# Loads and stores of half the partitions in pairs from one queue, in pieces of two slots, and a new hand-written order

## The chip, the cores and the metric

The kernel runs on one core of a Trainium2 chip. The metric is the device time of one execution in microseconds (us). A core has five engines with instruction streams of their own: TensorE (PE, matrix products; its weight loads are PEld), VectorE (DVE), ScalarE (ACT), GpSimd (POOL) and SyncE (SP), which here does nothing but issue transfers (DMAs). Each engine runs its instructions in the order in which they were issued, and waits on semaphores for the others.

## The reference

Two branches over S = 2048 tokens of D = 640 channels, mixed by a gate per token:

```python
x = A_q
g = _sigmoid((x * gate_w).sum(-1, keepdims=True))
a = _A_ref(x, A_k, A_v, A_shift_k, A_ssm_k, A_ssm_D)   # q * (longconv(kv, ssm_k) + kv*ssm_D)
b = _B_ref(x, B_w1, B_w2, B_w3, B_w4)
return g * a + (1 - g) * b
```

Branch A: `k_shift` is k convolved along the tokens with four taps per channel, `kv = k_shift * v`, then a causal convolution of kv along all 2048 tokens with `ssm_k` (by FFT in the reference), the term with `ssm_D`, and a product with q. Branch B: layer norm, `w1` (640 to 640), gelu, a shift of each quarter of the channels by 1, -1, 2 or -2 tokens, `w2`, a residual; layer norm, `w3` (640 to 1536), gelu, `w4`, a residual.

## The kernel before

**Layout.** Token t = 32 n + 16 g + s (g is 0 or 1, s from 0 to 15) lies on partition 64 g + n in slot s. So x, k, v, q and out are 128 partitions by 16 slots of 640 channels, and a transfer of one g covers half of the partitions: g = 0 the lower 64, g = 1 the upper 64. For one partition consecutive slots are contiguous in DRAM.

**Work.** `build` lists some 790 tasks. Names used below:

- `sin` and what precedes it make the tables of sines (TRIG). `cjb.j`/`cj.j` spread tap j over all partitions by a product with ones (PE, L464) and copy it out. `fill` holds one PSUM bank for products of zeros (L255), which the launcher issues where it expects PE to wait, so that its clock stays up.
- Branch B: `st1.s` (statistics of a slot: three instructions on DVE, or two activations on ACT), `rs1.s` (POOL), `nm1.s` (normalise), `tr1.s` (10 transposes for two slots, L540), `ev1`/`evh` (copies out of PSUM), `w1.G.p` (five products of 512 columns per part p of a group G of four slots, L615 and L619), `g1.G.p` (gelu on ACT), `w2.s` (L641), `x1.s` (residual, DVE L648), `sq.s`, `ve2`, `st2`, `nm2`, `dt2` (the second norm, with a transpose by DMA), `w3.c.f` (48 of them, L724), `g2`, `w4.s` (L738), `t2.s` (residual, DVE L744), `gate`, `gz`, `gg`.
- Branch A: `trh.cb` (32 transposes of the filter, L754; `evt` copies them out). For each group gi of four slots, from 3 down to 0: four tap products `kvgi.m3..m0` and three additions `kvgi.a2..a0` and the product with v, `kvgi.v` (L774, L778, L782; all on DVE, 128 x 2560). The convolution is a transform of two steps with a trip through DRAM between them: `s1h`/`s1x` (first step of filter and of kv, L809 and L822), `e1` copies, `wF` writes, `rF` reads, `s2` (L856), `e2`, `pa`/`pb` (products on DVE, L871), `s3` (back, L884), `e3`, `wG` writes, `rG` reads, `s4` (L934). `s2` of any part needs all of `wF`, so it needs `s1x.0` to `s1x.3`, which need `kv0.v`. Then `yq.s` (DVE L940) multiplies by q and the gate, `ad.s` (DVE L946) adds branch B, and `st` stores.

**Order.** `ORDER` is a list of task numbers written out by hand; a letter behind a number picks the engine (a: ACT, v: DVE, p: POOL). The tasks are issued in that order, so each engine gets its own sequence from it. `Plan.place` walks the list with assumed durations and chooses PSUM banks and other buffers, and how many products of zeros are put ahead of a PE task; it doesn't move a task.

**Transfers.** All go through `dma` on SP, but for the upper halves of x, which ACT issues. Eight completion semaphores are used in turn: the ninth transfer waits until the first of its turn has landed. Loads come in halves: x in six ranges of slots (two or four slots), k in four ranges of four slots, v in four, q and out in eight of two slots:

```python
for (s0, s1) in [(14, 16), (0, 2), (2, 4), (4, 8), (8, 12), (12, 14)]:
    for g in range(2):
        dma(f"ldx{s0}.{g}", ..., (nc.scalar if g else nc.sync).dma_start(...), queue="ACT" if g else "SP", ...)
```

Each half is a task of its own, and `ORDER` may set the two halves of a range far apart.

Of the kernel before, what the change touches and what calls it, by code (L numbers as in the profile page):

```python
# [16 lines left out]
P = 128  # L17
D = 640
# [23 lines left out]
403 455 48 113a 461 404 405 406 407 408 166 145 168 450a 172 462a 402 46 456a 169 173 443 444a 459 170 167 460a
146 401 171 53 174 152 445 147 447 457 175 153 52 409 414 410 148 458a 137 446a 448a 214 150 151 182 176 149 464
413 415 215 177 183 216a 463 179 180 140 157 451 452 185 143 217 465 473 158 220 163 181 186 159 474a 466a 188
471 416 189 412 164 411 469 477 196 50 221 470a 192 224v 225 218v 478v 472a 197 417 418 467 483 485 193 419 468a
190 486a 191 194 160 484a 154 420 481 161 219 476 165 479 475 195 198 222v 421 155 162 264 424 480a 482a 199 223
# [37 lines left out]
class Plan:  # L84
# [62 lines left out]
    def place(self, order):  # L147
        tasks = self.tasks
        n = len(tasks)
        free = {e: 0.0 for e in LAT}  # L150
# [71 lines left out]
def kernel(  # L222
# [16 lines left out]
    nc = tc.nc  # L239
# [8 lines left out]
    with tc.manual_schedule():  # L248
        nc.vector.memset(env.early("FZ", [P, 512], BF16)[:], 0.0)
# [104 lines left out]
def build(env, nc, io):  # L354
# [19 lines left out]
    def dma(name, nbytes, fn, issue=0.58, queue="SP", **kw):  # L374
        return add(name, queue, issue, fn, nbytes=nbytes, **kw)
# [79 lines left out]
    fill = add("fill", "PE", 0.02, lambda t: None, acq=[ONE], mode="f")  # L455
# [18 lines left out]
    for (s0, s1) in [(14, 16), (0, 2), (2, 4), (4, 8), (8, 12), (12, 14)]:  # L474
        for g in range(2):
            dma(f"ldx{s0}.{g}", 64 * (s1 - s0) * D * BF * 1.2, lambda t, s0=s0, s1=s1, g=g: (nc.scalar if g else nc.sync).dma_start(
                out=env["x"][64 * g:64 * g + 64, s0:s1, :], in_=qv[g, :, s0:s1, :]), queue="ACT" if g else "SP",
                w=[("x", s, g) for s in range(s0, s1)])
# [12 lines left out]
    for (i0, i1) in ((15, 19), (11, 15), (7, 11), (3, 7)):  # L491
        for g in range(2):
            dma(f"ldk{i0}.{g}", 64 * (i1 - i0) * D * BF * HALF, lambda t, i0=i0, i1=i1, g=g: nc.sync.dma_start(
                out=env["K"][64 * g:64 * g + 64, i0:i1, :], in_=kv_[g, :, i0 - 3:i1 - 3, :]),
                w=[("K", i, g) for i in range(i0, i1)], roles=("K",))
    dma("ldkh1", 64 * 3 * D * BF * 2, lambda t: nc.sync.dma_start(out=env["K"][64:128, 0:3, :], in_=kv_[0, :, 13:16, :]),
        w=[("K", i, 1) for i in range(3)], roles=("K",))
    dma("ldkh0", 64 * 3 * D * BF * 2, lambda t: nc.sync.dma_start(out=env["K"][1:64, 0:3, :], in_=kv_[1, 0:63, 13:16, :]),
        w=[("K", i, 0) for i in range(3)], roles=("K",))
# [265 lines left out]
    for gi in (3, 2, 1, 0):  # L765
        for g in range(2):
            dma(f"ldv{gi}.{g}", 64 * 4 * D * BF * HALF, lambda t, gi=gi, g=g: nc.sync.dma_start(
                out=env["VC"][64 * g:64 * g + 64, 0, :, :], in_=vv[g, :, 4 * gi:4 * gi + 4, :]), w=[("V", g)], roles=("VC",))
# [144 lines left out]
    for s0 in range(0, 16, 2):  # L913
# [4 lines left out]
        qown = None  # L918
        for g in range(2):
            def ldq(t, s0=s0, g=g, o=qown):  # L920
                b = (o or t).buf["Q"][0]
                nc.sync.dma_start(out=env["QO"][64 * g:64 * g + 64, 2 * b:2 * b + 2, :], in_=qv[g, :, s0:s0 + 2, :])
            kw = dict(acq=("Q",), after=("W12",)) if qown is None else {}
            t = dma(f"ldq.{s0}.{g}", 64 * 2 * D * BF * HALF, ldq, use=[qown] if qown else [], w=[("q", s0, g)], **kw)
            qown = qown or t
        oown = None
        for i in range(2):
# [14 lines left out]
            y = add(f"yq.{s}", "DVE", 0.88, yq, use=[t], rel=[(t, "U"), (qown, "Q")], r=["GG", ("q", s0, 0), ("q", s0, 1)], acq=("V",),  # L942
# [6 lines left out]
            o = add(f"ad.{s}", "DVE", 0.75, ad, use=[y] + ([oown] if oown else []), rel=[(y, "V")], r=["GG", ("x", s, 0), ("x", s, 1)],  # L949
                    w=[("o", s)], after=("W12",), **kw)  # L950
            oown = oown or o
        for g in range(2):
            def st(t, s0=s0, g=g, o=oown):
                b = 4 + 2 * o.buf["O"][0]
                nc.sync.dma_start(out=ov[g, :, s0:s0 + 2, :], in_=env["QO"][64 * g:64 * g + 64, b:b + 2, :])
            dma(f"st.{s0}.{g}", 64 * 2 * D * BF * HALF, st, r=[("o", s0), ("o", s0 + 1)], rel=[(oown, "O")])
# [32 lines left out]
```

## Time and profile before

| | us |
|---|---|
| median of 3 runs | 238.26 (238.21 to 238.35) |
| the profiled execution | 238.23 |
| its span, first to last instruction | 236.5 |
| outside the span | 1.73 |
| PE busy | 220.1 (93%) |
| DVE busy | 185.9 (79%) |
| ACT busy | 158.2 (67%) |
| POOL busy | 36.8 (16%) |

Transfers move 56.23 MB at a mean of 238 GB/s. The products of zeros count as busy time of PE: 27 of them, 9.7 us, all in the first 24 us. A busy share is an average over stages; which engine bounds a stage is read from the waits in it. PE's mean granted clock is 0.971.

### The profile page before, as it was taken

To read this page: it belongs to the slowest core of one execution; us is meant where nothing else is said; L and a number is where in the kernel's file an instruction comes from. 1 tells how busy PE (TensorE), PEld (TensorE's weight loads), DVE (VectorE), ACT (ScalarE), POOL (GpSimd) and SP (SyncE) were. 2 spreads that over 40 slices of the span, in tenths; PEclk is the share of its full clock that TensorE was granted. 3 is DMA by queue.
4 is the path that set the end of the run, shared out by engine and by line. 5 is a ranking of instruction groups with operands and counts; after the bars stand their busy time and mean duration, and the time that the engine had idled before them with its cause. 6 is when DMAs were issued, how large, how long until landed. Compare 5 with 4: busy or idle time off the path is not lost.

```text
span 236.5 us, 5276 instructions
## 1 busy us (share of the span) xinstructions
PE 220.1 (93%) x2135; PEld 109.7 (46%) x2154; DVE 185.9 (79%) x263; ACT 158.2 (67%) x221; POOL 36.8 (16%) x91
## 2 busy tenths in 40 slices
PE   8489799999999999999999999999879999999990
PEld 2147576634544564444554343334345654454550
DVE  6926696899999989996754888897999327787892
ACT  0995989998699797887963868897976702522000
POOL 8553364000530330000240000000000000000000
PEclk9679999999999989999999999999999999999997
DMA  6999999998998956985999699987851876877942
GB/s 169 206 224 286 288 214 194 229 335 309 358 243 197 257 199 160 271 236 149 320 259 387 205 237 276 259 283 269 262 192 36 316 258 238 294 218 244 266 112 55
DMA packets 37429, 56.23 MB, mean 238 GB/s; under 512 B 13467, under 2 KB 28572, under 8 KB 37404
## 3 DMA queue, kind: packets, MB, share of 16 engines
q1 hardware_dynamic: 36924, 54.57, 80.2%
q10 hardware_dynamic: 480, 1.31, 2.4%
q8 instruction: 17, 0.28, 0.5%
q14 instruction: 8, 0.07, 0.1%
HBM read 34.90 MB, written 18.35 MB: 225 GB/s over the span
## 4 chain that ended last, share of the span: by engine, by line
PE 76%; DMA 13%; DVE 3%; issue 2%; ACT 2%; SPq 1%; ACTq 0%; DVEq 0%
PE PS L724 23%; PE PS L738 16%; PE PS L641 9%; PE PS L615 8%; DMA x<-in_A_q_dram 6%; DMA W<-in_B_w_dram 5%; PE PS L884 4%; PE PS L856 4%; PE PS L809 4%; DMA QO<-in_A_q_dram 2%; PE PS L619 2%; PE PS L754 2%; PE PS L934 2%; DVE W L940 1%; PE PS L540 1%
## 5 line engine op out<-in xcount | busy, mean ns | idle before, releaser
L738 PE MATMUL PS<-W,h2T 128*128 128x128 bf16 (+1 forms) x372 | 53.6, 297 | 0.6
L731 ACT ACTIVATE h2T<-PS 128x512 bf16<-128x512 f32 x48 | 27.8, 605 | 29.6 <-PE PS L724 29.0
L738 PEld LDWEIGHTS <-h2T 128*128 128x128 bf16 x384 | 29.9, 98 | 25.9 <-issue 2.3
L379 ACT CAST FS<-PS 128x1024 bf16<-128x1024 f32 x36 | 35.1, 1017 | 3.6 <-PE PS L809 2.4
L724 PEld LDWEIGHTS <-W 128*128 128x128 bf16 x240 | 21.9, 99 | 30.2 <-issue 8.7
L379 ACT CAST XH<-PS 128x1024 bf16<-128x1024 f32 x26 | 25.6, 1018 | 5.9 <-PE PS L856 4.2
L724 PE MATMUL PS<-x1nT,W 128*128 128x512 bf16 x120 | 29.5, 392 | 0.0
L724 PE MATMUL PS<-XB,W 128*128 128x512 bf16 x120 | 28.3, 380 | 0.0
L774 DVE TENSOR_TENSOR VC<-K,VC 128x2560 bf16<-128x2560 bf16 x16 | 23.7, 1489 | 0.3
L871 DVE TENSOR_TENSOR PP<-XH 128x2048 bf16<-128x2048 bf16 x20 | 23.6, 1220 | 0.5 <-ACT XH L379 0.2
L744 DVE TENSOR_TENSOR x<-PS,x 128x640 bf16<-128x640 f32 x16 | 13.1, 822 | 13.4 <-PE PS L738 13.2
L641 PE MATMUL PS<-W,hsT 128*128 128x128 bf16 (+1 forms) x155 | 23.2, 302 | 0.3
L615 PE MATMUL PS<-xnT,W 128*128 128x512 bf16 x80 | 19.0, 380 | 0.4 <-DMA W<-in_B_w_dram 0.4
L698 POOL TENSOR_TENSOR r<-v,MH 128x2 f32<-128x2 f32 x8 | 8.9, 1107 | 64.7 <-DVE v L693 62.9
L381 DVE CAST XH<-PS 128x1024 bf16<-128x1024 f32 x14 | 16.8, 1221 | 2.7 <-PE PS L856 2.7
L778 DVE TENSOR_TENSOR VC<-VC 128x2560 bf16<-128x2560 bf16 x12 | 17.9, 1490 | 0.3
L940 DVE SCALAR_TENSOR_TENSOR W<-PS,GG,QO 128x640 bf16<-128x640 f32 x16 | 13.4, 880 | 6.0 <-PE PS L934 3.6
L641 PEld LDWEIGHTS <-hsT 128*128 128x128 bf16 x160 | 12.8, 100 | 11.5 <-issue 1.5
L379 ACT CAST GS<-PS 128x1024 bf16<-128x1024 f32 x14 | 13.9, 1016 | 3.2 <-PE PS L884 3.1
L856 PE MATMUL PS<-FX,TRIG 64*32 64x512 bf16 x320 | 12.9, 382 | 1.6 <-DVE GS L381 0.8
L648 DVE SCALAR_TENSOR_TENSOR x<-PS,x 128x640 bf16<-128x640 f32 x16 | 12.8, 819 | 1.0 <-PE PS L641 1.0
L946 DVE SCALAR_TENSOR_TENSOR QO<-x,OG,W 128x640 bf16<-128x640 bf16 x16 | 13.3, 879 | 0.1
(105 smaller groups left out, 266.8 us busy)
## 6 DMA issues: line engine op xcount, KB each, us to landing
FH<-FS SPq DMA_DIRECT2D x8, 640.0 KB, 5.6
FXD<-FS SPq DMA_DIRECT2D x8, 640.0 KB, 4.6
FX<-FH SPq DMA_DIRECT2D x10, 512.0 KB, 4.0
FX<-FXD SPq DMA_DIRECT2D x10, 512.0 KB, 6.0
GX<-GD SPq DMA_DIRECT2D x8, 640.0 KB, 5.2
W<-in_B_w_dram SPq DMA_DIRECT2D x2, 1920.0 KB, 17.4
GD<-GS SPq DMA_DIRECT2D x8, 480.0 KB, 3.7
SK<-in_A_ssm_k_dram SPq DMA_DIRECT2D x5, 512.0 KB, 7.6
```

The lines of the kernel that those rows point to most:

```text
L379: nc.scalar.copy(out=out, in_=in_)
L381: (nc.vector if t.on == "DVE" else nc.gpsimd).tensor_copy(out=out, in_=in_)
L615: nc.tensor.matmul(m[:, b, :], lhsT=W[:, 0, kb, 160 * fb:160 * fb + 128], rhs=rhs(kb, shifts[fb]), start=(kb == 0), stop=(kb == 4))
L641: nc.tensor.matmul(m[:, c0:c1], lhsT=env["hsT"][:, o.buf["hs"][0], fb, 128 * (s % 4):128 * (s % 4) + 128], rhs=env["W12"][:, 1, fb, c0:c1] ...
L724: nc.tensor.matmul(env.PS[:, t.buf["U"][0], :], lhsT=env["W3"][:, kb, 128 * fb:128 * fb + 128], rhs=env.nT(int(nP[-1]))[:, :, kb, :], star ...
L731: nc.scalar.activation(out=env["h2T"][:, o.buf["h2"][0], fb, :], in_=env.PS[:, t.buf["U"][0], :], func=ACT.Gelu_apprx_tanh)
L738: nc.tensor.matmul(m[:, c0:c1], lhsT=env["h2T"][:, o.buf["h2"][0], fb, 128 * (s % 4):128 * (s % 4) + 128], rhs=env["W4"][:, fb, c0:c1], st ...
L774: nc.vector.tensor_tensor(out=VC[:, o], in0=env["K"][:, a + 3 - j:a + 7 - j, :], in1=w, op=ALU.mult)
L778: nc.vector.tensor_tensor(out=VC[:, 1], in0=VC[:, 1], in1=VC[:, 2], op=ALU.add)
L856: nc.tensor.matmul(env.U(t.buf["U"][0])[32 * j:32 * j + 32, gp, :], lhsT=CRI()[64 * gp:64 * gp + 64, 32 * pc:32 * pc + 32], rhs=X[64 * gp: ...
L871: nc.vector.tensor_tensor(out=env["PP"][:, o.buf["PP"][0], a, :].rearrange("p (b c) -> p b c", b=2), in0=X.unsqueeze(1).broadcast_to([P, 2 ...
L940: nc.vector.scalar_tensor_tensor(out=u, in0=env.Uf(t.buf["U"][0])[:, 0:D], scalar=SS("GG")[:, s:s + 1], in1=env["QO"][:, 2 * q.buf["Q"][0] ...
```

## The change

**Halves.** A new helper issues both halves of a range back to back from SP, the upper half first, as one task:

```diff
-HALF = 1.45
+HALF = 1.1
+    def halves(name, nbytes, out, in_, **kw):
+        def fn(t):
+            for g in (1, 0):
+                nc.sync.dma_start(out=out(t, g), in_=in_(t, g))
+        return add(name, "SP", 1.08, fn, nbytes=nbytes, **kw)
-    for (s0, s1) in [(14, 16), (0, 2), (2, 4), (4, 8), (8, 12), (12, 14)]:
...
+    for s0 in (14, 0, 2, 4, 6, 8, 10, 12):
+        halves(f"ldx{s0}", P * 2 * D * BF * HALF, lambda t, g, s0=s0: env["x"][64 * g:64 * g + 64, s0:s0 + 2, :],
...
-    for (i0, i1) in ((15, 19), (11, 15), (7, 11), (3, 7)):
...
+    for i0 in (15, 17, 11, 13, 7, 9, 3, 5):
+        halves(f"ldk{i0}", P * 2 * D * BF * HALF, lambda t, g, i0=i0: env["K"][64 * g:64 * g + 64, i0:i0 + 2, :],
...
+    def kh0(t):
+        nc.sync.dma_start(out=env["K"][1:49, 0:3, :], in_=kv_[1, 0:48, 13:16, :])
+        nc.sync.dma_start(out=env["K"][49:64, 0:3, :], in_=kv_[1, 48:63, 13:16, :])
...
+        for h in range(2):
+            halves(f"ldv{gi}.{h}", P * 2 * D * BF * HALF, lambda t, g, h=h: env["VC"][64 * g:64 * g + 64, 0, 2 * h:2 * h + 2, :],
...
+        qown = halves(f"ldq.{s0}", ..., acq=("Q",), w=[("q", s0)], after=("W12",))
+        halves(f"st.{s0}", ..., r=[("o", s0), ("o", s0 + 1)], rel=[(oown, "O")])
```

x goes from 12 transfers (6 on SP, 6 on ACT) to 16 on SP, k from 8 to 16 plus one for the split of `ldkh0`, v from 8 to 16; q and out stay at 16 each, now two by two. ACT issues none.

**Zeros.** The memset of the zeros becomes a task (`zeros`, on DVE, behind one small memset), and at least one product of zeros is put ahead of each `cjb`:

```diff
+                    if self.kept is not None and t.name[:3] == "cjb":
+                        t.fill = max(t.fill, 1)
-        nc.vector.memset(env.early("FZ", [P, 512], BF16)[:], 0.0)
+    zeros = add("zeros", "DVE", 0.3, lambda t: nc.vector.memset(env.early("FZ", [P, 512], BF16)[:], 0.0), roles=("C0",))
```

The assumed durations of `ad` (0.75 to 0.88) and of the first free moment of SP (0 to 0.58) change too; they act on `place` alone.

**Order.** `ORDER` is new as a whole, and the numbers stand for other tasks, since there are 769 instead of 788. Read back into names, the sequences begin like this (a name of a half pair stands for two transfers after the change):

```
SP before  ldD ldx14.1 ldx14.0 ldCJ ldx0.1 ldx2.0 ldx2.1 ldx12.1 ldx8.1 ldx4.1 ldx0.0 ldgw ldsk0 ldw2b0 ldw2b3 ldw2b2
 (and ACT) ldsk3 ldx4.0 ldw2b1 ldsk4 ldx12.0 ldsk2 ldw1 ldx8.0 ldsk1 ldw2a ldk15.0 ldk7.1 ldk11.1 ldk3.1 ldk15.1
           ldkh0 ldk11.0 ldk3.0 ldv3.1 ldk7.0 ldv3.0 ldw4 ldw3 wFh.4.1 ...
SP after   ldx0 ldsk2 ldCJ ldx14 ldx4 ldsk4 ldx2 ldD ldsk3 ldw2b3 ldsk1 ldsk0 ldx6 ldw1 ldgw ldk17 ldw2b0 ldx8 ldw2b2
           ldx10 ldx12 ldkh1 ldk15 ldv3.0 ldk13 ldk7 ldk5 ldw2a ldkh0 ldv3.1 ldw2b1 ldk11 ldk3 ldw3 wFh.4.0 wFh.4.1 ...
PE before  fill cjb x4 trh.0 trh.3 tr1.2 tr1.14 tr1.0 trh.2 w1.0.0 tr1.4 w1.0.2 trh.4 trh.1 w1.0.4 w1.0.1 w1.0.3 tr1.6
           tr1.12 w2.0 w2.2 w2.1 tr1.8 ...
PE after   fill cjb x4 trh.4 trh.2 trh.3 tr1.0 tr1.14 trh.0 trh.1 tr1.2 tr1.4 w1.0.0 w1.0.2 s1h.4 s1h.6 w1.0.4 w1.0.3
           s1h.0 s1h.1 tr1.6 w1.0.1 s1hr.0 s1h.3 w1.1.0 tr1.8 w1.1.2 s1h.7 s1hr.4 w1.1.4 w1.1.1 w1.1.3 s1h.2 s1h.5
           w2.2 w2.0 w2.5 w2.4 w2.3 ...
DVE before ... evt.4 evh.0 nm1.7 nm1.13 st1.10 ev1.6 st1.11 dfold x1.0 x1.2 x1.1 nm1.10 nm1.11 ev1.8 x1.3
           kv3.m3 kv3.m2 kv3.a2 ...
DVE after  ... evt.1 st1.8 nm1.7 dfold st1.9 nm1.8 nm1.6 kv3.m2 ev1.6 nm1.9 st1.12 st1.11 ev1.8
           kv3.m3 kv3.a2 kv3.m1 kv3.a1 kv3.m0 x1.2 x1.0 x1.5 ...
ACT before st1.15 st1.3 cj.3 cj.2 cj.0 cj.1 sin evt.0 st1.5 ev1.14 evt.3 evt.2 st1.6 g1.0.0 ...
ACT after  st1.0 st1.1 cj.2 cj.0 cj.3 sin evt.4 evt.2 st1.4 nm1.3 ev1.14 evt.0 st1.6 ev1.4 g1.0.0 ...
```

Around the first of the last four slots of kv, `s1x.0`, PE's order changes too. Ahead of it stood, before, w3.0.8, w3.1.0, w3.1.5, w3.1.10 and w4.1; they now stand behind it, and no task goes the other way. On DVE 58 tasks stood from kv3.m3 to kv0.v (32 of kv, 12 x1, 6 nm2, 5 ve2, e1h, gz, gg); now 53 (31 of kv, 15 x1, 2 nm1, 2 ve2, ev1, gz, nm2). In the section from the first s2 to the last s3 PE has 16 w3 and 4 w4 besides before, and 23 w3 and 4 w4 after. PE's sequence changes the shape of its products 101 times before and 118 times after, 62 and 72 of them behind `s1x.0`.

More of the change, by code (lines that the diff above doesn't have):

```diff
@@ L42 @@
[L42 to L46, printed above, removed]
@@ new lines @@
+73v 396a 52 37 393 392a 71v 33 66v 35 34 55v 81v 74 65v 24 79a 56v 67 394v 28 57 68v 69v 19 72 76a 40 75v 58a
+59v 387 389 388a 82 84v 30 89v 87a 25 80 32 90 83v 88 77 85 86a 26 27 78v 119 120 390v 123 47 124 39 450 454
+451a 455a 398 127 95v 96 92v 125 397 438 97v 42 99v 91v 440 126 43 441a 46 128 439a 93 29 121 122 446 447a 98
+401 94v 444 100v 141 142 111v 101 145 456 105v 48 445a 102v 146 457a 458 149 150 459a 399 31 41 400 106 143 147
+148 112 442 144 402 403 404 405 452 453a 113a 45 114 135 136 129 154 151 103a 115a 49 130 155 108v 138 443a 104
@@ new lines @@
+286 552a 287 545 582 556 310 554a 281 558 288 308 583 557v 559a 585 560 561 271 304 282 311 325 571 586a 584v
+572 272 326 562 312 210 277 566 573v 567 587 343 564a 569 315 278 563v 568a 588 316 574 575a 603 619 630 570v
+589a 590 614 323 329 324 576 591v 707 577 330 546 350 331 547v 620 592 548a 332 615 617 333 635 317 618a 616v
+593 621a 334 318 578 579a 313 580v 598 314 622 604 606 549 605a 319 623a 327 624 599 320 344 345v 646 651 607v
+328 594 695 351v 600a 581 625 631 595v 696v 596a 633 321 632v 601 565 634a 602a 636 283 637v 626 322 597 638 284
@@ L66 @@
+639a 608 609 628a 335 353v 627a 662 663 664a 640 336 610 612a 641 611a 678 289 667 652 654 347v 275 655a 613
+653v 647 649 650a 341 629 648v 668 290 656 665 269 276 657 666a 342 679 681 279 683 680a 270 280 669v 346 658
+348 660a 682v 672 670 293 671a 684 659a 673 685a 642 643a 294 644v 674 354 686 676a 661 687a 688 689 675a 337
+338 690 691v 339 645 295 692a 677 693 352 340 291 296 355 697 702 292 699 363 703 700 706 708 733 701 715 711
[4 rows of a table added]
 """
@@ L149, in place @@
         n = len(tasks)
-        free = {e: 0.0 for e in LAT}
+        free = {e: 0.0 if e != "SP" else 0.58 for e in LAT}
         bufs = {p: [0.0] * k for p, k in self.pools.items()}
@@ L372, in build, with dma @@
         qv, kv_, vv, ov = tok(q2), tok(k2), tok(v2), tok(o2)
-    def dma(name, nbytes, fn, issue=0.58, queue="SP", **kw):
-        return add(name, queue, issue, fn, nbytes=nbytes, **kw)
+    def dma(name, nbytes, fn, issue=0.58, **kw):
+        return add(name, "SP", issue, fn, nbytes=nbytes, **kw)
+    def halves(name, nbytes, out, in_, **kw):
[3 more added lines that the diff above has]
+        return add(name, "SP", 1.08, fn, nbytes=nbytes, **kw)
     def copy(t, out, in_):
@@ L453, in build @@
     add("sin", "ACT", 3.5, c_sin, r=["pha", "c0"], w=["TRIG"], roles=("PRE", "C0"))
-    fill = add("fill", "PE", 0.02, lambda t: None, acq=[ONE], mode="f")
+    zeros = add("zeros", "DVE", 0.3, lambda t: nc.vector.memset(env.early("FZ", [P, 512], BF16)[:], 0.0), roles=("C0",))
+    fill = add("fill", "PE", 0.02, lambda t: None, use=[zeros], acq=[ONE], mode="f", roles=("C0",))
     dma("ldCJ", 5120, lambda t: nc.sync.dma_start(out=env.early("CJR", [1, 4 * D], BF16), in_=io["sk"].rearrange("d j -> (d j)").unsqueeze(0)),
@@ L471, in build @@
                                                   in_=io["gw"].rearrange("(t p) -> p t", p=P)), w=["GW"])
-    for (s0, s1) in [(14, 16), (0, 2), (2, 4), (4, 8), (8, 12), (12, 14)]:
[L475 to L478, printed above, removed]
+    for s0 in (14, 0, 2, 4, 6, 8, 10, 12):
+        halves(f"ldx{s0}", P * 2 * D * BF * HALF, lambda t, g, s0=s0: env["x"][64 * g:64 * g + 64, s0:s0 + 2, :],
+               lambda t, g, s0=s0: qv[g, :, s0:s0 + 2, :], w=[("x", s, g) for s in (s0, s0 + 1) for g in range(2)])
     dma("ldw1", 819200, lambda t: nc.sync.dma_start(out=env["W12"][:, 0], in_=io["w1"].rearrange("(t p) n -> p t n", p=P)),
@@ L490, in build @@
             w=[("SK", cb)], roles=("SK",))
-    for (i0, i1) in ((15, 19), (11, 15), (7, 11), (3, 7)):
[L492 to L496, printed above, removed]
+    for i0 in (15, 17, 11, 13, 7, 9, 3, 5):
+        halves(f"ldk{i0}", P * 2 * D * BF * HALF, lambda t, g, i0=i0: env["K"][64 * g:64 * g + 64, i0:i0 + 2, :],
+               lambda t, g, i0=i0: kv_[g, :, i0 - 3:i0 - 1, :], w=[("K", i, g) for i in (i0, i0 + 1) for g in range(2)], roles=("K",))
+    dma("ldkh1", 64 * 3 * D * BF * HALF, lambda t: nc.sync.dma_start(out=env["K"][64:128, 0:3, :], in_=kv_[0, :, 13:16, :]),
         w=[("K", i, 1) for i in range(3)], roles=("K",))
-    dma("ldkh0", 64 * 3 * D * BF * 2, lambda t: nc.sync.dma_start(out=env["K"][1:64, 0:3, :], in_=kv_[1, 0:63, 13:16, :]),
-        w=[("K", i, 0) for i in range(3)], roles=("K",))
+    def kh0(t):
+        nc.sync.dma_start(out=env["K"][1:49, 0:3, :], in_=kv_[1, 0:48, 13:16, :])
+        nc.sync.dma_start(out=env["K"][49:64, 0:3, :], in_=kv_[1, 48:63, 13:16, :])
+    dma("ldkh0", 64 * 3 * D * BF * HALF, kh0, issue=1.08, w=[("K", i, 0) for i in range(3)], roles=("K",))
     dma("ldw3", 1966080, lambda t: nc.sync.dma_start(out=env["W3"][:], in_=io["w3"].rearrange("(t p) n -> p t n", p=P)), w=["W3"])
@@ L765, in build @@
     for gi in (3, 2, 1, 0):
-        for g in range(2):
-            dma(f"ldv{gi}.{g}", 64 * 4 * D * BF * HALF, lambda t, gi=gi, g=g: nc.sync.dma_start(
-                out=env["VC"][64 * g:64 * g + 64, 0, :, :], in_=vv[g, :, 4 * gi:4 * gi + 4, :]), w=[("V", g)], roles=("VC",))
+        for h in range(2):
+            halves(f"ldv{gi}.{h}", P * 2 * D * BF * HALF, lambda t, g, h=h: env["VC"][64 * g:64 * g + 64, 0, 2 * h:2 * h + 2, :],
+                   lambda t, g, gi=gi, h=h: vv[g, :, 4 * gi + 2 * h:4 * gi + 2 * h + 2, :], w=[("V", h)], roles=("VC",))
         a = 4 * gi
@@ L917, in build @@
         ld = dma(f"rG.{s0}", P * 5120, rg, issue=0.5, r=[("G", m) for m in range(10)], acq=("GX",), after=("FX",))
[L918 to L925, printed above, removed]
+        qown = halves(f"ldq.{s0}", P * 2 * D * BF * 1.3, lambda t, g: env["QO"][64 * g:64 * g + 64, 2 * t.buf["Q"][0]:2 * t.buf["Q"][0] + 2, :],
+                      lambda t, g, s0=s0: qv[g, :, s0:s0 + 2, :], acq=("Q",), w=[("q", s0)], after=("W12",))
         oown = None
@@ L941, in yq @@
                                                in1=env["QO"][:, 2 * q.buf["Q"][0] + i, :], op0=ALU.mult, op1=ALU.mult)
-            y = add(f"yq.{s}", "DVE", 0.88, yq, use=[t], rel=[(t, "U"), (qown, "Q")], r=["GG", ("q", s0, 0), ("q", s0, 1)], acq=("V",),
+            y = add(f"yq.{s}", "DVE", 0.88, yq, use=[t], rel=[(t, "U"), (qown, "Q")], r=["GG", ("q", s0)], acq=("V",),
                     after=("C0",))
@@ L948, in build @@
             kw = dict(acq=("O",)) if oown is None else {}
-            o = add(f"ad.{s}", "DVE", 0.75, ad, use=[y] + ([oown] if oown else []), rel=[(y, "V")], r=["GG", ("x", s, 0), ("x", s, 1)],
+            o = add(f"ad.{s}", "DVE", 0.88, ad, use=[y] + ([oown] if oown else []), rel=[(y, "V")], r=["GG", ("x", s, 0), ("x", s, 1)],
                     w=[("o", s)], after=("W12",), **kw)
             oown = oown or o
[L952 to L956, printed above, removed]
+        halves(f"st.{s0}", P * 2 * D * BF * 1.3, lambda t, g, s0=s0: ov[g, :, s0:s0 + 2, :],
+               lambda t, g, o=oown: env["QO"][64 * g:64 * g + 64, 4 + 2 * o.buf["O"][0]:6 + 2 * o.buf["O"][0], :],
+               r=[("o", s0), ("o", s0 + 1)], rel=[(oown, "O")])
     pl.close()
```

31 lines of the change are left out of this document (11 added, 20 removed), and 8 rows, old and new, of the table ORDER.

## The prediction

> **What bounds the kernel now.** I read the busy times by stage first.
>
> ```profile
> core 0: us, PE busy (x) PEld busy (x) DVE busy (x) ACT busy (x) POOL busy (x), PEclk, DMA share, GB/s
> 0.00:27.00 27.00, 19.66 (x161) 11.34 (x163) 18.04 (x49) 17.68 (x23) 14.94 (x46) 0.87 0.95 225
> 27.00:160.00 133.00, 132.52 (x1245) 63.86 (x1254) 112.48 (x154) 111.03 (x164) 21.85 (x46) 0.99 0.91 255
> 160.00:180.00 20.00, 17.74 (x324) 8.60 (x327) 17.54 (x17) 16.08 (x19) 0.00 (x0) 1.00 0.63 212
> 180.00:216.00 36.00, 35.84 (x303) 18.07 (x304) 23.05 (x27) 13.42 (x18) 0.00 (x0) 1.00 0.75 253
> 216.00:230.50 14.50, 14.37 (x110) 7.84 (x110) 12.98 (x17) 0.00 (x0) 0.00 (x0) 1.00 0.64 179
> 230.50:236.50 6.00, 0.00 (x0) 0.00 (x0) 1.77 (x3) 0.00 (x0) 0.00 (x0) 0.72 0.23 55
> ```
>
> From 27 us on PE idles 3.0 us in all (0.48 + 2.26 + 0.16 + 0.13), so PE bounds the kernel from there to its last product at 230.5. In the first 27 us it is busy for 19.66, of which 9.7 are zeros: some 17 us without useful work. The last 6.0 us are the last residual, sum and stores. The chain of waits says what that start waits for:
>
> ```profile
> 5.06 9.59 DMA x<-in_A_q_dram
> ...
> 16.20 10.76 DMA W<-in_B_w_dram
> 26.96 0.05 issue
> 27.01 1.25 PE PS L615 x5
> ```
>
> w1's first products wait for W1, which lands at 26.96, late in a transfer queue with a DMA share near 1. Next, the timelines of DVE and of PE around branch A:
>
> ```profile
> 45.60 2.89 DVE L774 TENSOR_TENSOR VC<-K,VC 128x2560 bf16<-128x2560 bf16 x2
> ...
> 107.87 1.49 DVE L782 TENSOR_TENSOR K<-VC 128x2560 bf16<-128x2560 bf16 x1 [0.88 <-DMA VC<-in_A_v_dram]
> ```
> ```profile
> 111.31 0.82 PE L809 MATMUL PS<-K,TRIG 64*128 64x512 bf16 x6
> ```
>
> DVE works from kv3.m3 at 45.60 to the end of kv0.v at 109.36, 63.8 us with 0.88 of waiting. PE reaches s1x.0, which needs kv0.v, at 111.31. So DVE is second in line by only 1.95 us: a PE that runs ahead gains that much, and no more unless DVE's chain ends earlier. Last, what halves move at, from the stages table of other stretches:
>
> ```profile
> 2.50:6.00 3.50, 3.50 (x12) 1.21 (x11) 2.87 (x11) 0.43 (x1) 3.34 (x10) 1.00 1.00 271
> 30.00:36.00 6.00, 6.00 (x90) 4.51 (x91) 5.80 (x15) 5.36 (x11) 4.34 (x12) 1.00 1.04 213
> 36.00:42.00 6.00, 5.95 (x53) 3.73 (x53) 3.85 (x9) 5.64 (x7) 2.33 (x6) 1.00 1.03 198
> 50.00:56.00 6.00, 6.00 (x61) 2.27 (x61) 5.86 (x5) 5.18 (x9) 0.00 (x0) 1.00 1.06 386
> ```
>
> The last column is GB/s, the one before the DMA share; all four are saturated. From 30 to 42 us halves of k come in runs of one half: about 205. From 2.5 to 6 upper and lower halves of x come mixed, from two queues: 271. From 50 to 56 whole weights: 386.
>
> **The change part by part.**
>
> *The start of PE.* Up to and with W1, 5.38 MB stood in the queue; now 5.12 MB. ACT issued x until 5.53 and ran its first activation at 6.86, behind a table load of 1.28; x's first pair lands at about 4.6 (as in before: 4.40 for its first pair), and the table load needs no data, so ACT starts up to 2.3 us earlier. Both let w1.0.0 start at 24 to 26 instead of 27.01, I take 25, and by then two more trh (3.7 us, from L754's 3.77 for two) and tr1.4 (0.6) are done. PE's work from w1.0.0 to s1x.0 was 84.3 us (27.01 to 111.31). It loses these 4.3 and the five tasks that go behind s1x.0: four w3 (1.10 each, 5.50 for 25 products in the chain) and a w4 (3.3), 7.7. Left are 72.3: with no wait PE would be at s1x.0 at 97.3.
>
> *k and DVE.* DVE's kv3.m3 now needs slots 11 to 14, so pair ldk11, behind 10.00 MB in the queue (before, 10.08 MB had landed at 47.99 by the trace's landings). From 47.9 I subtract: k and v up to there, 2.62 MB, at 271 instead of 205 (12.8 to 9.7): 3.1. Half of x, 1.3 MB, came in runs of upper halves: 1.5. Three filter loads now stand in a row, 1.57 MB: at 386 instead of the 225 of 10 to 20 us they would save 2.9; they still share the ports with x around them, so half, 1.5. Sum 6.1: S, the start of kv3.m3, is 41.8. Bounds: none of it (47.9), and all of it with the other half of x too (38.8). DVE alone would be there at 38.4 (ldk13, behind 7.75 MB, at about 37.0 less 4.5, then 5.9 us: kv3.m2 1.49, ev1 twice 0.82, nm1 0.43, two st1 of 1.17), so it would wait 3.4 us. What queues behind that wait: x1.2, which frees the bank pair that PE's fifth w2 needs. It ends five kv operations later, at 41.8 + 7.5 + 0.8 = 50.1; PE would be there at 25 + 20.4 (ten w1, ten s1h, two tr1, four w2) = 45.4. PE waits 4.7 and comes to s1x.0 at 102.0.
>
> From kv3.m3 to kv0.v DVE had 63.8. One kv operation (1.49), five nm2 (2.2), three ve2 (0.9), e1h (1.22) and gg (0.34) go, three x1 (2.5), two nm1 (0.9) and ev1 (0.82) come: 61.9. x1.12 and x1.13 come so soon that they may wait for PE's w2, 0 to 1.5, I take 0.8. kv0.v ends at 41.8 + 61.9 + 0.8 = 104.5, after PE's 102.0: **s1x.0 now waits for DVE**, and runs at 104.7.
>
> *From s1x.0 to the end.* Before: 230.47 - 111.31 = 119.2. Added: the five tasks, 7.7. Ten more changes of shape in PE's sequence: a stretch of s2 costs 0.34 for 8 products and 0.77 for 24, so 0.125 for the stretch; two changes make one stretch, 0.6 to 1.25, I take 0.9. In the transform section PE idled 2.36 us (55.64 busy of 128 to 186, DVE 49.65); seven w3 more there (7.7) against some 4.8 us more on DVE should remove half of it: -1.2, bounds 0 and -2.4. Sum 119.2 + 7.7 + 0.9 - 1.2 = 126.6.
>
> *Edits at nothing.* SP issues 27 more transfers at about 0.5: 14 us of a queue that waits for some 140 us in its own waits view; 51 must go before ldk11 is complete, 26 us of 41.8. Without that cover each would cost its 0.5. Eight in flight at 164 KB are 1.3 MB, 4.8 us at 271, more than the 3.0 of x's quickest landing. One product of zeros ahead of each tap product is at most 4 x 0.61; PE waited 3.45 for ACT there, and even 2.4 us late would end in PE's wait for x1.2. The memset moves by about 0.3 on a DVE that waits for x soon after. q and out keep their 16 + 16 transfers, and the last stores their two. v in more pieces: 0 to 1 us, DVE waited 0.88 for it once already. ldkh0 is needed only by the last taps.
>
> *Sum.* 41.8 + 61.9 + 0.8 + 0.2 + 126.6 = 231.3 for PE's end; with 6.0 and the 1.73 outside the span 239.0, against 238.23 of the profiled execution (0.03 under the median). The break-even is S at 41.0.
>
> **The rivals.** *Early k (faster).* Pairs run well above 271 (202 to 206 us, q and out, moves 340), all terms count, S is 39.0; DVE hardly waits, and the transform section loses all its idle time: 239.0 - 2.8 - 1.2 = 235.0. For it: PE's 17 useless us at the start, and a timing that only 2.8 us of transfers decide. Against: the row at 2.5 to 6 had two queues, this has one, where a run of one half can still form.
>
> *Halves serialise (slower).* If pairs on one queue still move at 205, only the filter's 1.5 is saved, S is 46.4 and the time 239.0 + 4.6 = 243.6; it decides as soon as pairs stay under about 240 GB/s. The rows of 30 to 42 speak for it, those of 2.5 to 6 against. The Trainium skill, DMA: Bandwidth & Descriptors, Rules for kernel authors, says this of transfers to disjoint partition halves: "Don't bother — they serialize"; by that rule the time is this rival's. The trace agrees for runs of one half and not for mixed ones (271 against 205).
>
> *New stalls in the transform section (slower).* DVE's 54.5 us and the copies on ACT sit in a section of some 64; with two buffers each for the s2 results and products, its waits could double rather than halve: +2.4 + 1.2, 242.6.
>
> **How the numbers follow.** Forecast 0.42, early k 0.33, serialised halves 0.12, transform stalls 0.13. The forecast's own range is S from 40.4 to 43.4: 237.6 to 240.6. Measurement tells 0.2%, 0.48 us, from no change: of the forecast's 0.42, 0.05 are faster, 0.11 the same, 0.26 slower. Faster: 0.05 + 0.33 = 0.38; same 0.11; slower 0.26 + 0.12 + 0.13 = 0.51. The range reaches from the fast rival at 235.0, slightly below for its own unknowns, to the transform rival at 242.6: 234.6 to 242.6, leaving out most of the serialised case.
>
> **What would show it.** In the changed profile: W1 landed before 26 us and w1.0.0 at 24 to 26; DVE's L774 after its first operation waits on K, and five operations in a row start at about 41.8; PE waits at L641 for an x1 near 45 to 50; and at L809, near 102 to 105, for L782. If PE finds kv0.v done at s1x.0, the forecast is wrong, and so it is if the k pairs land at 205 GB/s or over 300, or if PE idles over 2.4 us between s2 and s3.

## The result and the profile after

The changed kernel takes 239.96 us (median of 12 runs), the kernel before 237.73 (12 runs beside them): a ratio of 1.0105, interval 1.0068 to 1.0141, so about 1% slower. The prediction said 239.0 and slower. Against the kernel before, it had forecast 0.8 us more; found are 1.8 for the profiled executions and 2.2 for the medians. The profiled execution took 240.0, with a span of 238.2. Here and below medians are of all executions, while ratios leave out those in a second, slower state of the chip, into which the profiled executions of the first two experiments fell.

The same stages as before (columns as there; the last stretch shown ends with PE's last product, now at 232.4):

```profile
core 0: us, PE busy (x) PEld busy (x) DVE busy (x) ACT busy (x) POOL busy (x), PEclk, DMA share, GB/s
0.00:27.00 27.00, 24.85 (x246) 15.82 (x247) 20.64 (x51) 21.36 (x28) 17.07 (x48) 0.94 0.89 252
27.00:160.00 133.00, 126.34 (x1229) 57.49 (x1228) 112.08 (x152) 108.74 (x163) 24.68 (x43) 0.99 0.86 256
160.00:180.00 20.00, 20.00 (x259) 9.06 (x265) 15.49 (x16) 14.42 (x18) 0.00 (x0) 1.00 0.52 159
180.00:216.00 36.00, 36.00 (x324) 17.47 (x300) 23.20 (x28) 11.95 (x17) 0.00 (x0) 1.00 0.77 255
216.00:232.40 16.40, 15.74 (x122) 8.31 (x120) 13.57 (x18) 0.60 (x1) 0.00 (x0) 1.00 0.53 148
```

The start is better: PE is busy for 24.85 us of the first 27, not 19.66. Of that, 10.6 are products of zeros (34 of them), 9.7 before, so the useful work there rose from some 10 to some 14 us. The transform stage is better too: no idle time from 160 to 180, where there were 2.26 us. But from 27 to 160 PE now idles 6.7 us, where it had idled 0.5. The view of PE's waits names them:

```profile
PE PS L650 <- DVE x L657: 3.6, 1, 3.6
PE PS L818 <- DVE xnT L390: 1.5, 1, 1.5
...
PE PS L865 <- DMA FX<-FH: 1.2, 1, 1.2
...
PE PS L818 <- DVE K L791: 0.3, 1, 0.3
```

The first is `w2.3` waiting for `x1.2`, the second an `s1h` behind `kv3.m2`, the last `s1x.0` for `kv0.v`. The chain of waits shows what stands behind them (start, length, engine and line; SPq is SP issuing a transfer):

```profile
5.42 5.77 DMA SK<-in_A_ssm_k_dram
...
12.99 9.37 DMA GW<-in_gate_w_dram
22.99 0.59 SPq L383
...
31.24 0.60 SPq L383
35.94 6.68 DMA K<-in_A_k_dram
42.64 1.50 DVE VC L783
...
50.16 0.84 DVE x L657 x2
51.03 4.57 PE PS L650 x20
...
103.76 1.50 DVE K L791
105.31 0.61 PE PS L818 x4
```

From 13 to 36 us it runs over SP. W1, which lands at 21.82, holds a semaphore turn, and SP issues nothing from 19.75 until then. Then one issue follows another, until the second half of ldk11 goes out at 35.94 and lands at 42.6. (The chain names the gate weights, issued right behind W1, whose small load lands at 22.36. But SP's timeline has no gap behind 21.84, so their turn cost nothing.) SP's timeline at W1's turn, and DVE's at `kv3.m3`:

```profile
18.20 1.55 SPq L493 DMA_DIRECT2D W<-in_B_w_dram  x1
21.84 2.38 SPq L383 DMA_DIRECT2D x<-in_A_q_dram  x4
```
```profile
42.64 1.49 DVE L783 TENSOR_TENSOR VC<-K,VC 128x2560 bf16<-128x2560 bf16 x1 [4.06 <-DMA K<-in_A_k_dram]
```

DVE's `kv3.m3` starts when k has landed. It had been ready 4.06 us earlier. Everything up to `x1.2` comes behind it, and PE stands. After that stall PE's clock is low for 4 us (PE alone; busy, granted clock, DMA share, GB/s):

```profile
50.00:52.00 2.00, 0.96 (x4) 0.94 1.06 397
52.00:54.00 2.00, 2.00 (x10) 0.50 1.06 361
54.00:56.00 2.00, 2.00 (x20) 0.70 1.08 361
```

That is 1.0 + 0.6 us more. (Before had a dip of the same worth at 86 to 90, 0.58 and 0.57, without such a stall. So from 27 to 160 us the mean clock is 0.99 in both, and that the stall caused this dip is not shown.) The rates of the pairs:

```profile
2.50:6.00 3.50, 3.39 (x12) 1.22 (x11) 3.22 (x14) 1.37 (x2) 3.33 (x8) 1.00 0.96 303
22.00:30.00 8.00, 8.00 (x91) 4.81 (x90) 7.36 (x18) 7.16 (x11) 3.47 (x10) 1.00 0.79 216
28.00:32.00 4.00, 4.00 (x39) 1.23 (x37) 2.50 (x8) 3.99 (x6) 2.42 (x6) 1.00 0.98 253
30.00:36.00 6.00, 4.48 (x39) 1.97 (x36) 3.30 (x6) 6.00 (x8) 1.14 (x3) 1.00 0.96 271
```

From 28 to 32 little but pairs is under way (until 29.3 also ldkh1, 240 KB): 253 GB/s, and 271 and 303 in the rows where other loads lie between them. Runs of one half, in pieces of four slots, had moved at 198 to 213. From 22 to 30 the share is only 0.79: there the transfers wait for SP.

### The profile page after: what moved, and what is told of

It reads as the page before. It is cut to its first block, busy times and chain, and to the rows that moved or that the text cites. A ratio compares the mean times of both kernels' runs of the same rounds, so it can differ in the third digit from the quotient of the medians.

```text
span 238.2 us, 5341 instructions
## 1 busy us (share of the span) xinstructions
PE 222.9 (94%) x2159; PEld 108.1 (45%) x2159; DVE 186.7 (78%) x262; ACT 157.1 (66%) x224; POOL 41.7 (18%) x90
## 4 chain that ended last, share of the span: by engine, by line
PE 60%; DMA 17%; DVE 10%; SPq 8%; issue 2%; ACT 1%; DVEq 0%; ACTq 0%
PE PS L747 21%; PE PS L733 15%; SPq L383 6%; PE PS L650 6%; PE PS L865 5%; DMA GW<-in_gate_w_dram 4%; PE PS L893 4%; PE PS L624 4%; DVE VC L787 4%; DMA GX<-GD 4%; DVE VC L783 3%; DMA K<-in_A_k_dram 3%; DMA FX<-FH 3%; DMA SK<-in_A_ssm_k_dram 2%; PE PS L937 2%
## 5 line engine op out<-in xcount | busy, mean ns | idle before, releaser
L747 PE MATMUL PS<-W,h2T 128*128 128x512 bf16 (+1 forms) x384 | 53.9, 300 | 0.0
L388 ACT CAST FS<-PS 128x1024 bf16<-128x1024 f32 x38 | 37.3, 1023 | 3.4 <-PE PS L818 2.4
L733 PEld LDWEIGHTS <-W 128*128 128x128 bf16 x240 | 21.0, 98 | 30.5 <-issue 9.3
L388 ACT CAST XH<-PS 128x1024 bf16<-128x1024 f32 x25 | 24.9, 1014 | 9.4 <-PE PS L865 8.5
L733 PE MATMUL PS<-XB,W 128*128 128x512 bf16 x120 | 29.0, 381 | 0.0
L650 PE MATMUL PS<-W,hsT 128*128 128x512 bf16 (+1 forms) x160 | 25.1, 313 | 3.6 <-DVE x L657 3.6
L733 PE MATMUL PS<-x1nT,W 128*128 128x512 bf16 x120 | 28.1, 380 | 0.0
L880 DVE TENSOR_TENSOR PP<-XH 128x2048 bf16<-128x2048 bf16 x20 | 24.2, 1221 | 2.8 <-ACT XH L388 1.6
L390 DVE CAST XH<-PS 128x1024 bf16<-128x1024 f32 x15 | 18.2, 1221 | 3.9 <-PE PS L865 2.5
L707 POOL TENSOR_TENSOR r<-v,MH 128x2 f32<-128x2 f32 x8 | 7.8, 978 | 68.2 <-DVE v L702 56.5
```

The costliest lines, as they stand in the source:

```text
L388: nc.scalar.copy(out=out, in_=in_)
L390: (nc.vector if t.on == "DVE" else nc.gpsimd).tensor_copy(out=out, in_=in_)
L650: nc.tensor.matmul(m[:, c0:c1], lhsT=env["hsT"][:, o.buf["hs"][0], fb, 128 * (s % 4):128 * (s % 4) + 128], rhs=env["W12"][:, 1, fb, c0:c1] ...
L733: nc.tensor.matmul(env.PS[:, t.buf["U"][0], :], lhsT=env["W3"][:, kb, 128 * fb:128 * fb + 128], rhs=env.nT(int(nP[-1]))[:, :, kb, :], star ...
L747: nc.tensor.matmul(m[:, c0:c1], lhsT=env["h2T"][:, o.buf["h2"][0], fb, 128 * (s % 4):128 * (s % 4) + 128], rhs=env["W4"][:, fb, c0:c1], st ...
L880: nc.vector.tensor_tensor(out=env["PP"][:, o.buf["PP"][0], a, :].rearrange("p (b c) -> p b c", b=2), in0=X.unsqueeze(1).broadcast_to([P, 2 ...
```

## The experiments

My theory: the arrival of k for `kv3.m3` sets `s1x.0`, through DVE's chain and through `x1.2` and PE; and k comes late for its place in SP's queue, not for its rate. The rivals: PE's stall is a loss by itself; what lies behind `s1x.0` sets the end; the transfers' rate sets k's arrival. A part of the changes below is a new place in `ORDER`, told in the names of tasks.

**k earlier.** Order in SP's queue:

```diff
-ldkh1 ldk15 ldv3.0 ldk13 ldk7 ldk5 ldw2a ldkh0 ldv3.1 ldw2b1 ldk11 ldk3
+ldk15 ldk13 ldk11 ldv3.0 ldkh1 ldk7 ldk5 ldw2a ldkh0 ldv3.1 ldw2b1 ldk3
```

> Only the order in SP's queue differs from the changed kernel: ldk11 is issued right behind ldk13, and ldv3.0, ldkh1, ldk7, ldk5, ldw2a, ldkh0, ldv3.1 and ldw2b1 come after it. Theory (the arrival of k for kv3.m3 holds DVE's chain to s1x.0 and, through x1.2, PE): kv3.m3 starts when DVE is ready, at 37 to 39 instead of 42.64; PE's wait for x1.2 falls from 3.6 us to under 1; s1x.0 starts at 101 to 102.5 instead of 105.3; the time is 2.5 to 4 us under the changed kernel's 239.96, so 236 to 237.5. Rival (what lies behind s1x.0 sets the end): s1x.0 comes earlier, but the us gained there are given back as waits in the transform section, and the time is within 0.7 us of 239.96.

Measured: 237.27 us, ratio to the kernel before 0.9963 (0.9920 to 1.0005). `kv3.m3` starts at 37.51 without a wait. But `s1x.0` comes at 104.26 only, a gain of 1.05 us. PE's waits, and the one on its timeline:

```profile
PE PS L650 <- DMA W<-in_B_w_dram: 3.4, 2, 3.0
```
```profile
46.68 7.76 PE L650 MATMUL PS<-W,hsT 128*128 128x512 bf16 x46 [3.02 <-DMA W<-in_B_w_dram]
```

The old wait is replaced by one for W2, whose last part I had moved behind more loads: it lands at 46.64. The time is as expected, the way to it is not: a second load is as urgent as k.

**x1 earlier on DVE.**

```diff
-kv3.m3 kv3.a2 kv3.m1 kv3.a1 kv3.m0 x1.2 x1.0
+kv3.m3 kv3.a2 x1.2 kv3.m1 kv3.a1 x1.0 kv3.m0
```

> Only DVE's order differs from the changed kernel: x1.2 runs behind kv3.a2 and x1.0 behind kv3.a1, instead of both behind the five kv3 operations. Both kernels give DVE the same work up to kv0.v. Theory (DVE's chain from kv3.m3 to kv0.v sets s1x.0): PE's wait of 3.6 us for x1.2 goes, but comes back at s1x.0 as a wait of 3 to 5.5 us for kv0.v; s1x.0 stays at 105 +- 0.5 and the time within 0.5 us of 239.96. Rival (PE's stall at w2 and the lower clock behind it are the loss themselves): the time falls by 3.6 to 5.3 us, to 234.7 to 236.4.

Measured: 240.66, ratio 1.0080 (1.0033 to 1.0127), against 1.0105 for the changed kernel; `s1x.0` at 105.43. The stall of 3.6 broke up into waits of 1.50, 1.07 and 0.71. The rival's 234.7 to 236.4 did not come, so the stall is not the whole loss by itself: with k late, PE loses the time in one place or another. The wait did not come back at `s1x.0`, as I had expected (0.34 there). In this profile k came later still (`kv3.m3` at 44.84, not 42.64) and `s1x.0` hardly so; whether the new place of x1 wins back a part of the stall, these runs don't tell, since the intervals of the two ratios overlap.

**k first, W2 next.** As the first experiment, and ldw2a and ldw2b1 right behind ldk11:

```diff
-ldk15 ldk13 ldk11 ldv3.0 ldkh1 ldk7 ldk5 ldw2a ldkh0 ldv3.1 ldw2b1 ldk3
+ldk15 ldk13 ldk11 ldw2a ldw2b1 ldv3.0 ldkh1 ldk7 ldk5 ldkh0 ldv3.1 ldk3
```

> As e1_k_early, with ldw2a and ldw2b1 put right behind ldk11 in SP's queue, ahead of ldv3.0, ldkh1, ldk7 and ldk5. In e1_k_early kv3.m3 started at 37.5 as expected, but PE then waited 3.4 us for W2a and W2b1, and s1x.0 came only 1.05 us earlier than in the changed kernel. Theory (the order of the loads in SP's queue is what costs: k, then W2): both waits are gone, PE idles under 1 us between 27 and 60, s1x.0 starts at 99.5 to 101 instead of 105.3, and the time is 234 to 236, faster than before. Rival (PE and DVE wait for each other at x1 and w2 whatever the loads do): DVE's waits for PE's w2 grow to over 3 us again, s1x.0 stays later than 103 and the time is 236.5 or more.

Measured: 234.51 us, ratio 0.9873 (0.9831 to 0.9915): faster than both kernels. PE's largest waits, then `kv3.m3` on DVE and `s1x.0` on PE:

```profile
PE PS L865 <- DMA FX<-FH: 1.5, 1, 1.5
PE PS L256 <- DVE C L464: 1.2, 1, 1.2
PE PS L865 <- DMA FX<-FXD: 0.7, 1, 0.7
```
```profile
37.73 1.48 DVE L783 TENSOR_TENSOR VC<-K,VC 128x2560 bf16<-128x2560 bf16 x1
```
```profile
99.09 0.60 PE L818 MATMUL PS<-K,TRIG 64*128 64x512 bf16 x4 [0.34 <-DVE K L791]
```

PE waits nowhere between 27 and 99 us. `s1x.0` is 6.2 us earlier than in the changed kernel. The same code, the same transfers, the same order on PE and DVE: a few places changed in one queue turn 1% slower into 1.3% faster. The first theory stands, with W2 beside k.

**One transfer for each pair.** For the loads of x, k, v and q:

```diff
-            for g in (1, 0):
-                nc.sync.dma_start(out=out(t, g), in_=in_(t, g))
+            for g in (None,) if name[:2] == "ld" else (1, 0):
+                nc.sync.dma_start(out=out(t, g), in_=in_(t, g))
```

(g = None: all 128 partitions, from a source with the two halves as its outermost dimension.)

> As the changed kernel, but each pair of halves of x, k, v and q is one transfer of 128 partitions instead of two of 64; same bytes, same order, 36 issues fewer on SP, 21 of them ahead of ldk11's last. Theory (SP's issuing, 0.64 us for each half, back to back from 21.8 to 36.5 us, sets when k lands): ldk11 lands at 34 to 38 instead of 42.6, kv3.m3 starts at 36 to 39, and the time falls by 2.5 to 4 us to 236 to 237.5. Rival (the transfers themselves set it, at some 270 GB/s whatever the number of issues): ldk11 lands within 1 us of 42.6 and the time stays within 0.5 us of 239.96. A second rival (a transfer over all partitions of such a source is no faster than one half): rates near 205 GB/s in the same stretches, ldk11 later than 44, slower than 241.

Measured: 379.51 us, ratio 1.597 (1.590 to 1.604). All three expectations missed. A stretch in which nothing but such loads ran, and SP's part of the chain there:

```profile
69.00:75.00 6.00, 0.00 (x0) 0.00 (x0) 0.00 (x0) 0.00 (x0) 0.00 (x0) 0.50 0.13 51
```
```profile
68.97 6.36 SPq L387
75.37 7.02 SPq L387
82.44 6.22 SPq L387
```

51 GB/s at a share of 0.13, which is 2 of 16 DMA engines, and each issue takes 6 to 7 us of SP instead of 0.6. The Trainium skill, DMA: Bandwidth & Descriptors, Why a DMA increments its semaphore by 16 and not by 1, says that the number of engines is the largest up to 16 that divides the slowest dimension on both sides; for a source whose slowest dimension is 2 that gives 2, and the trace agrees. So in this form one transfer can't stand in for a pair, and the run, which was to test SP's pace, says nothing on it.

**W1 from ACT's queue.** One load issued by another engine:

```diff
-    dma("ldw1", 819200, lambda t: nc.sync.dma_start(out=env["W12"][:, 0], ...
+    dma("ldw1", 819200, lambda t: nc.scalar.dma_start(out=env["W12"][:, 0], ..., queue="ACT", ...
```

> As the changed kernel, but W1 is issued from ACT, just ahead of its sine, instead of from SP. Theory (SP is held: its issue behind W1 waits for the semaphore turn that W1 holds until it lands at 21.8, and from there 23 issues of 0.64 us set when k lands): SP is not held at 21.8, the DMA share from 22 to 30 us rises from 0.8 to over 0.9, ldk11 lands 1.5 to 4 us earlier than 42.6, and the time falls by 1 to 3 us to 237 to 239. Rival (eight in flight or the bytes set the pace, whichever engine issues): ldk11 lands within 1 us of 42.6 and the time is within 0.5 us of the changed kernel.

Measured: 242.08, ratio 1.0180 (1.0136 to 1.0224), so neither. The semaphores' turns run over both queues. W1 took a turn at 9.18 and SP met it sooner, with the next half of x. SP's timeline, and the transfers in the gap:

```profile
9.82 2.31 SPq L497 DMA_DIRECT2D SK<-in_A_ssm_k_dram  x2
19.07 1.11 SPq L383 DMA_DIRECT2D x<-in_A_q_dram  x2
```
```profile
18.00:22.00 4.00, 4.00 (x56) 3.22 (x55) 0.90 (x1) 2.23 (x6) 1.77 (x5) 1.00 0.33 87
```

SP stands from 12.1 until W1 lands at 19.06, the transfers run dry (share 0.33), `kv3.m3` comes at 45.07 instead of 42.64 (+2.4), `s1x.0` at 107.70 (+2.4), and the median is 2.1 us longer. This was not the test that I had meant. It shows the hold of SP; what the hold costs it does not show, since with a change as small as the lower half first (below) `kv3.m3` came at 44.95 and the ratio was 1.0160.

**The small edits undone.** Lower half first, no zeros at the taps, ldkh0 as one transfer; then the first two of them alone; then the changed kernel again as their measure:

```diff
-            for g in (1, 0):
+            for g in (0, 1):
-                    if self.kept is not None and t.name[:3] == "cjb":
-                        t.fill = max(t.fill, 1)
-        nc.sync.dma_start(out=env["K"][1:49, 0:3, :], in_=kv_[1, 0:48, 13:16, :])
-        nc.sync.dma_start(out=env["K"][49:64, 0:3, :], in_=kv_[1, 48:63, 13:16, :])
+        nc.sync.dma_start(out=env["K"][1:64, 0:3, :], in_=kv_[1, 0:63, 13:16, :])
```

> The changed kernel with three of its small edits undone at once: the lower half is issued first again, no product of zeros is forced ahead of each tap product, and ldkh0 is one transfer again. The prediction put all of these at nothing: the time stays within 0.5 us of 239.96, kv3.m3 within 0.7 us of 42.6 and w1's first product within 0.4 of 26.1. Rival (the zeros keep PE's clock up, or the order of the halves counts): w1's first product later than 26.5, or a time that differs by over 0.7 us.

> As the changed kernel, with the lower half of each pair issued first, as before. e4_small_undone (three small edits undone at once) was about 0.9% slower than the changed kernel. If the order of the halves is the cause, this one is at 241 to 242.5 with kv3.m3 near 44; if not, it stays within 0.5 us of 239.96.

> As the changed kernel, without the product of zeros forced ahead of each tap product. If the zeros at the taps are the cause of e4_small_undone's 0.9%, this one is at 241 to 242.5, with a lower granted clock from 10 to 18 us and w1's products later than 26.5; if not, it stays within 0.5 us of 239.96, and what is left is ldkh0 in two transfers.

> The changed kernel itself once more, beside the next two, as the measure for e4_small_undone, e7_lower_first and e8_no_tap_zeros (1.016 to 1.020 of the kernel before). If the small edits are worth nothing, this comes out near those three, 1.013 to 1.020; if they are worth the 0.5 to 0.9% that those runs suggest, it stays at 1.0105 or less.

Measured: all three undone 1.0198 (1.0147 to 1.0248); lower half first 1.0160 (1.0116 to 1.0205); no zeros 1.0179 (1.0130 to 1.0228); the changed kernel again 1.0130 (1.0066 to 1.0193). The intervals overlap with the last, so at the size that these runs can tell, some 0.6%, the edits are worth nothing or a little to the good. (Against the changed kernel's first 1.0105, up to 1.0141, all three undone lies just outside, from 1.0147.) Which of them, if any, stays open.

**The halves alone, in the old order.** The changed code with the order of before (x's pairs where SP had issued the lower half, the others where the second half had stood).

> The changed kernel's code (pairs of halves from one queue, pieces of two slots, zeros) in the old order: x's pairs stand where SP issued the lower halves, k's, q's and the stores' where the second half of each was issued. Theory (pairs move faster than runs of halves, but the old order did not wait for k): between 30 and 42 us the transfers run at over 240 GB/s instead of 198 to 213, k's slots 11 to 14 land at least 3 us earlier than in the kernel before, kv3.m3 starts within 1.5 us of the 45.6 of before all the same, and the time is within 1.2 us of the kernel before. Rival (SP's 27 more issues are not hidden): W1 or the filter lands later, w1's first product comes after 28.5, and the time is 1.5 us or more above the kernel before. Rival (halves of one pair still serialise): 205 GB/s in the same stretch.

Measured: 251.25, ratio 1.0594 (1.0542 to 1.0645), for a reason of my own making. PE's waits:

```profile
PE PS L256 <- DVE C L464: 12.8, 1, 12.8
```

The memset of the zeros is now a step of DVE's order, and I had put it behind statistics that wait for x; PE's first product needs it. With it first:

> e10_halves_alone with the memset of the zeros as DVE's first step, where the kernel before has it. In e10_halves_alone it stood behind statistics that wait for x, and PE, which needs the zeros for its first product, waited 12.8 us for it. Theory (the pairs are worth little in the old order, because its DVE does not wait for k): PE starts at 1 to 1.5 us, w1's first product runs at 24.5 to 27.5, k's slots 11 to 14 land before 40 instead of at 46 to 48, kv3.m3 still starts at 43.5 to 46, and the time is 236 to 239, within 1.2 us of the kernel before. Rival (SP's further issues or the new shape of x's arrival hold the start): w1's first product after 28, over 1.5 us slower than the kernel before.

Measured: 237.51, ratio 1.0006 (0.9966 to 1.0046). W1's products and `kv3.m3`, with its neighbour ahead:

```profile
26.29 2.31 PE L624 MATMUL PS<-xnT,W 128*128 128x512 bf16 x5 [1.83 <-DMA W<-in_B_w_dram]
```
```profile
45.65 0.82 DVE L657 SCALAR_TENSOR_TENSOR x<-PS,x 128x640 bf16<-128x640 f32 x1 [0.28 <-PE PS L650]
46.40 2.89 DVE L783 TENSOR_TENSOR VC<-K,VC 128x2560 bf16<-128x2560 bf16 x2
```

Pairs by themselves are worth nothing in the old order: `kv3.m3` stands behind `x1` there and never waited for k. (It came at 46.40, slightly later than expected.) The rate expected of the pairs, over 240 GB/s from 30 to 42 us, was not reached throughout: 200 from 30 to 36 and 232 from 36 to 42, at shares of 0.90 and 0.85, so with SP holding them back again.

**The new order alone.** The code of before in the new order: k in pieces of four slots, x's upper halves from ACT.

> The kernel before (old pieces, x's upper halves from ACT, no zeros added) in the new order: each of k's four-slot pieces goes as its two halves one behind the other at the place of the first of the new pairs that kv3 needs, so slots 11 to 14 go where ldk13 stood. Theory (what the change loses is the place and the issue pace of k's second pair): with fewer SP issues ahead of it, the slots for kv3.m3 land before DVE is ready, kv3.m3 starts at 37 to 39.5, PE's wait for x1.2 is under 1.5 us, s1x.0 starts at 99.5 to 102.5 and the time is 234 to 237.5, under both kernels. Rival (the new order needs the small pieces): kv3.m2 and the steps behind it on DVE start more than 3 us later than 33.2, PE waits there, and the time is 239 or more.

Measured: 250.70, ratio 1.0535 (1.0472 to 1.0599): the theory missed. The chain:

```profile
8.78 7.10 DMA x<-in_A_q_dram
...
31.68 10.10 DMA x<-in_A_q_dram
```

These are upper halves of x, issued from ACT at 8.78 and 31.68, because in the new order x's loads stand among ACT's own work, and ACT takes them in turn. The rival's signs came (kv3.m2 at 45.25, PE waiting 5.8 us, over 239), but not by its cause, the piece size, on which the run tells nothing: it shows that the new order does not go with upper halves of x issued by ACT. The halves without the order make no difference; the order without the halves, with x so issued, is 5% slower.

## Why the prediction was right, step by step

The sum can be tried on each run. By the prediction's terms the time is 239.0 - 41.8 = 197.2 us plus S, the start of `kv3.m3`. Profiled executions:

| run | S | 197.2 + S | its time |
|---|---|---|---|
| changed kernel | 42.64 | 239.8 | 240.0 |
| the same again | 43.63 | 240.8 | 240.3 |
| x1 earlier | 44.84 | 242.0 | 241.5 |
| three small edits undone | 43.95 | 241.2 | 241.3 |
| lower half first | 44.95 | 242.2 | 242.2 |
| no tap zeros | 44.01 | 241.2 | 242.3 |
| W1 from ACT | 45.07 | 242.3 | 241.8 |
| k, then W2 first | 37.73 | 234.9 | 234.8 |
| k first, W2 late | 37.51 | 234.7 | 238.3 |

In eight of nine the sum is within 1.1 us, and in the ninth W2 breaks its condition.

Five of these are the changed kernel and its near copies (the first two rows, three small edits undone, lower half first, no tap zeros). Their S goes from 42.64 to 44.95, and the time goes with it. SP goes on behind W1 at 21.84, 23.41, 22.98, 22.95 and 23.28 in them, and S follows 20.2 to 22.0 us later. So the forecast's S of 41.8 is earlier than each of the five, and its break-even of 41.0 lay only 0.8 below it. The mechanism is the one forecast; that the sign and the size came out so near is in part luck.

- **The start of PE**: w1.0.0 at 26.14, forecast 24 to 26. W1 landed at 21.82, but the transposes (and five products of zeros) ahead of w1.0.0 lasted until 26.1, so an earlier W1 was partly lost. ACT's first activation came at 5.92, 0.94 us earlier than before and not up to 2.3: its table load waited for x as well, until 4.62.
- **S, 41.8 forecast, 42.64 found.** The sum is nearly right, its working only in part. Early pairs were faster than the 271 I took (303 from 2.5 to 6), and later SP was slower.
- **"Edits at nothing": SP.** This is the step that failed. I hid SP's 27 further issues behind its idle time over the whole kernel, and wrote that eight in flight are enough. In the trace SP issues back to back from 21.84 to 36.5, 0.64 us for 160 KB (256 GB/s at most), and before that it is held by the turns of the filter and of W1. Most of its free time lies later. No run changed the pace alone, so its price is read from the trace and not shown by a run.
- **DVE's chain**: 61.9 + 0.8 forecast, 62.6 found (42.64 to 105.25). But the trace's chain runs over PE from 51 to 84, and PE was only 0.33 us ahead at `s1x.0`, not 2.5: 1.1 us of later start, the `s1h` wait of 1.52 and the low clock were not in my sum, against 1.1 us less at `x1.2` (3.59 for 4.7). The two meet at `x1.12`, which waits 0.23 us for `w2.12` in the changed kernel; `s1x.0` follows it by 18.05 us there and in the runs with x1 earlier and with k, then W2 first, and by 18.06 with k first.
- **From `s1x.0` to the end**: 126.6 forecast, 127.05 found; PE idles 1.2 us from 128 to 186, as forecast (2.36 less 1.2); another 0.6 us is a wait of s4.
- **Rivals.** *Early k* was spent by the order in SP's queue and by SP's pace. With k, then W2 first its S of 39.0 is met (37.73), and the time is 234.5 where it was given 235.0; what it lacked was the queue, not the rate. *Halves serialise* is refuted, if closely: 253 GB/s for pairs alone, over its bound of 240, and near what SP's pace allows (256). The Trainium skill (DMA: Bandwidth & Descriptors, Rules for kernel authors) has the rule that transfers to disjoint partition halves serialize; read as this rival reads it, the trace disagrees for halves that alternate (253 GB/s, against 198 to 213 for runs of one half). *Transform stalls* did not come in the changed kernel.

## What to carry to other kernels

Where one queue issues everything, the order in that queue is a schedule of its own: rank its loads by the time at which an engine will stop for them, and look again when one is served, since the next (here W2) takes its place. A queue's idle time counts only in the stretch where its issues are due; count issues there, and look which slow transfer holds a completion semaphore that a later one needs (here W1).

## What was not expected of the hardware

- A load of 128 partitions whose source has the two halves as its outermost dimension ran at 51 GB/s on a DMA share of 0.13, and held SP for 6 to 7 us; as two transfers of 64 the loads move at 253 GB/s.
- The load of the gate weights, 1280 bytes by single elements, took 9.37 us to land behind W1 with its 800 KB (9.5); the two halves of k behind it took 9.0 and 8.6. A small load issued behind a large one waited as long as the large one.
- Upper and lower halves in turn on one queue moved a fifth or more faster than runs of one half (253 against 198 to 213 GB/s, all at a share near 1). The runs of one half were in pieces of four slots, the pairs in pieces of two. With the new order alone, where mostly halves of four slots came in turn, it was 232 GB/s from 28 to 32 at a share of 1.04. So how much of the gain is the turn and how much the size stays open.
- After a stall of 3.6 us PE's granted clock was 0.50 and 0.70 for 4 us; the kernel before had 0.58 and 0.57 over 4 us without such a stall.
